# From chunk 8 on, keys and queries are transposed by VectorE in 32x32 blocks, instead of by TensorE with ScalarE's copies

## Chip, cores, metric

One core of one Trainium2 chip. The metric is device time in microseconds; each figure is the median of several runs. The kernel before takes 741.78 us (4 runs, 740.48 to 742.51).

## The reference, cut to what matters

A retention recurrence over 768 positions for 4 batches x 8 heads, then a feed-forward layer on the 3072 tokens it gives:

```python
for t in range(S):
    state = gamma * state + einsum('bhd,bhe->bhde', k[:, :, t], v[:, :, t])
    y[:, :, t] = scale * einsum('bhd,bhde->bhe', q[:, :, t], state)
# ... y becomes x (3072 x 512), then
h = x @ w_in                       # 512 -> 2048
g = h * erf(softplus(h))
out = g @ w_out                    # 2048 -> 512
```

Everything is float32.

## The kernel before

The recurrence is done in chunks of 128 positions, 24 in all (6 a batch). Keys and queries of a chunk are scaled by decay factors (by GpSimd from chunk 7 on), transposed on TensorE into PSUM and copied out by ScalarE:

```python
    def ret_scale(j):                       # K_
        ...
        by = kq_s[:, j % NC, :, :, None].to_broadcast([P, 2, H, D])
        engine = nc.vector if j <= JPC + 2 else nc.gpsimd
        engine.tensor_tensor(KQ[j], KQ[j], by, op=ALU.mult)          # L346

    def ret_transpose(j):                   # T
        for i, (name, store) in enumerate((("k", KT), ("q", QT))):
            p = ret_psum()
            for u in range(HP):             # 4 transposes of 128x128 each
                nc.tensor.transpose(p[:, u, :], ..., ident)          # L355
            store[j] = ret.tile([P, HP, C], F32, name=name + "T")
            nc.scalar.copy(store[j], p)                              # L361
```

The main loop runs over half token pairs ("steps" g = 4 to 23; each does half of the hidden units for 256 tokens, as seven products with sums and differences in place of eight). One chunk of the recurrence (j = g + 2) is threaded through each step as long as there are chunks. The order of one step, for all engines alike:

```python
        hidden_part(g, 1); hidden_part(g, 2)     # part 2 ends with L567 on VectorE
        if put is not None:                      # every second step: results of the
            for step in range(4):                # last token pair go out
                put_part(put, step)              # ScalarE copy, then L637..L646 on VectorE
            put = None
        if more: T(j)
        hidden_part(g, 6)
        if more: S_(j); M(j)                     # scores; mask = L380 on VectorE
        hidden_part(g, 5)                        # reuses the bank that L567 reads
        if more: O_(j)                           # L403/L408, into the banks L380 reads
        hidden_part(g, 7)
        if more: U(j); A(j); ret_scale(j + 1)    # state product, state addition
        ...                                      # x_sums (L534), projections, parts 4, 3
        gate(g)                                  # ScalarE: softplus, then Erf (L451)
        ...                                      # more projections on TensorE
        gated(g); g_sums(g)                      # VectorE: 2 x L470, 4 x L594
```

What one step's `gated` and `g_sums` ask of VectorE is carried out at the start of the next step, when Erf is done.

## Time and profile before

| what | before |
|---|---|
| median | 741.78 us |
| profiled span | 739.9 us |
| TensorE busy | 723.5 us (98%) |
| one main-loop step (from one Erf end to the next) | 29.38 us |

A step's length is the difference of two successive ends of the Erf activation in the timeline. In the kernel before it repeats to 0.01 us from step to step. Two kinds of step must be told apart: "output steps" (odd g from 7 on, with the three VectorE additions L637 to L646 ahead of the mask) and the others. In the kernel before both take 29.38 us, since TensorE is full in both. (Steps whose chunk begins or ends a batch are 0.6 or 0.8 us shorter, as they lack some products.)

### The profile page before, as it was taken

To read this page: it belongs to the slowest core of one execution; us is meant where nothing else is said; L and a number is where in the kernel's file an instruction comes from. 1 tells how busy PE (TensorE), PEld (TensorE's weight loads), DVE (VectorE), ACT (ScalarE), POOL (GpSimd) and SP (SyncE) were. 2 spreads that over 40 slices of the span, in tenths; PEclk is the share of its full clock that TensorE was granted. 3 is DMA by queue.
4 is the path that set the end of the run, shared out by engine and by line. 5 is a ranking of instruction groups with operands and counts; after the bars stand their busy time and mean duration, and the time that the engine had idled before them with its cause. 6 is when DMAs were issued, how large, how long until landed. Compare 5 with 4: busy or idle time off the path is not lost.

```text
span 739.9 us, 11780 instructions
## 1 busy us (share of the span) xinstructions
PE 723.5 (98%) x5260; PEld 609.1 (82%) x5260; DVE 352.4 (48%) x461; ACT 274.3 (37%) x320; POOL 34.9 (5%) x30
## 2 busy tenths in 40 slices
PE   7889999999999999999999999999999999999997
PEld 6644444576999999999999999999999999999995
DVE  3999999955543332531631532433414424243314
ACT  2354562415334144244242341542442423414440
POOL 1000010010101101101001011011010100000000
PEclk9999999999999999999999999999999999999999
DMA  9999653021201201302202022112021000000000
GB/s 190 207 242 233 151 159 114 0 45 57 44 15 29 72 1 43 73 1 43 72 1 43 33 41 43 50 23 45 28 45 38 7 29 2 1 29 1 1 29 28
DMA packets 87522, 42.71 MB, mean 58 GB/s; under 512 B 76208, under 2 KB 76208, under 8 KB 87472
## 3 DMA queue, kind: packets, MB, share of 16 engines
q1 hardware_dynamic: 83920, 41.16, 24.0%
q10 hardware_dynamic: 3552, 0.80, 0.6%
q8 instruction: 41, 0.67, 0.4%
q14 instruction: 9, 0.07, 0.0%
HBM read 35.66 MB, written 6.29 MB: 57 GB/s over the span
## 4 chain that ended last, share of the span: by engine, by line
PE 79%; DVE 12%; DMA 4%; issue 2%; SPq 2%; ACT 1%; DVEq 0%; ACTq 0%
PE hp L551 34%; PE o L611 32%; PE r L368 3%; PE r L408 2%; PE r L355 2%; DVE w_out_sb L199 2%; DVE w_out_sb L201 2%; PE o L494 2%; DMA w_in_sb<-in_moe_w_in_dram 2%; DMA kq<-in_k_dram 2%; PE r L422 1%; DVE w_out_sb L197 1%; PE r L403 1%; DVE w_in_sb L191 1%; DMA v<-in_v_dram 1%
## 5 line engine op out<-in xcount | busy, mean ns | idle before, releaser
L551 PE MATMUL hp<-xs,w_in_sb 128*128 128x128 f32 x1280 | 159.4, 278 | 0.0
L551 PEld LDWEIGHTS hp<-xs,w_in_sb 128*128 128x128 f32 x1280 | 150.5, 192 | 7.0 <-issue 3.6
L611 PE MATMUL o<-w_out_sb,h 128*128 128x256 f32 x640 | 141.6, 379 | 0.0
L470 DVE TENSOR_TENSOR e<-h,e 128x1024 f32<-128x1024 f32 x44 | 51.9, 1221 | 180.0 <-ACT e L451 180.0
L611 PEld LDWEIGHTS o<-w_out_sb,h 128*128 128x128 f32 x640 | 121.6, 190 | 16.5
L551 PE MATMUL hp<-xT,w_in_sb 128*128 128x128 f32 x960 | 113.7, 275 | 0.0
L551 PEld LDWEIGHTS hp<-xT,w_in_sb 128*128 128x128 f32 x960 | 111.9, 192 | 1.9 <-issue 1.0
L611 PE MATMUL o<-w_out_sb,e 128*128 128x256 f32 x480 | 111.8, 382 | 0.9 <-DVE e L470 0.9
L611 PEld LDWEIGHTS o<-w_out_sb,e 128*128 128x128 f32 x480 | 88.2, 190 | 12.6 <-DVE e L470 1.3
L450 ACT ACT_TABLE_LOAD x24 | 30.8, 1283 | 91.2 <-PE o L611 89.1
L481 PE MATMUL hp<-xT,w_in_sb 128*128 128x512 f32 x128 | 58.4, 609 | 0.0
L346 POOL TENSOR_TENSOR kq<-kq,kq_s 128x1024 f32<-128x1024 f32 x17 | 32.7, 1925 | 534.4 <-DMA kq<-in_q_dram 469.8
L574 DVE TENSOR_TENSOR h<-h,hp 128x512 f32<-128x512 f32 x20 | 13.7, 687 | 86.4 <-ACT h L572 86.4
L579 DVE TENSOR_TENSOR h<-h,hp 128x512 f32<-128x512 f32 x20 | 13.7, 687 | 72.3 <-PE hp L551 72.3
L481 PEld LDWEIGHTS hp<-xT,w_in_sb 128*128 128x128 f32 x128 | 24.4, 196 | 28.7 <-issue 27.9
L413 ACT COPY xT<-r 128x256 f32<-128x256 f32 x44 | 14.4, 375 | 78.8 <-PE r L408 78.8
L450 ACT ACTIVATE e<-h 128x2048 f32<-128x2048 f32 x22 | 42.0, 1910 | 0.2
L451 ACT ACTIVATE e<-e 128x2048 f32<-128x2048 f32 x22 | 42.0, 1910 | 0.2
L577 ACT COPY h<-hp 128x512 f32<-128x512 f32 x20 | 11.7, 585 | 72.4 <-PE hp L551 72.4
L380 DVE TENSOR_TENSOR am<-r,causal 128x512 f32<-128x512 f32 x44 | 28.4, 683 | 18.3 <-PE r L368 17.0
L451 ACT ACT_TABLE_LOAD x24 | 30.8, 1283 | 0.4
L355 PE MATMUL r<-ident,kq 128*128 128x128 f32 x176 | 23.5, 275 | 5.8 <-DVE kq L346 5.5
(91 smaller groups left out, 656.3 us busy)
## 6 DMA issues: line engine op xcount, KB each, us to landing
w_out_sb<-in_moe_w_out_dram SPq DMA_DIRECT2D x14, 512.0 KB, 5.2
kq<-in_k_dram SPq DMA_DIRECT2D x24, 256.0 KB, 3.2
v<-in_v_dram SPq DMA_DIRECT2D x24, 256.0 KB, 4.2
w_in_sb<-in_moe_w_in_dram SPq DMA_DIRECT2D x12, 512.0 KB, 7.4
out_dram<-r SPq DMA_DIRECT2D x24, 256.0 KB, 2.3
kq<-in_q_dram SPq DMA_DIRECT2D x21, 256.0 KB, 4.0
w_out_sb<-in_moe_w_in_dram SPq DMA_DIRECT2D x4, 512.0 KB, 8.5
w_in_sb<-in_moe_w_out_dram SPq DMA_DIRECT2D x2, 512.0 KB, 4.1
```

What stands on the lines that cost most here:

```text
L199: nc.vector.scalar_tensor_tensor(lowf, lo, 2.0**-52, lowf, op0=ALU.mult, op1=ALU.mult)
L201: nc.vector.tensor_tensor(lowf, topf, lowf, op=ALU.add)
L346: engine.tensor_tensor(KQ[j], KQ[j], by, op=ALU.mult)
L355: nc.tensor.transpose(p[:, u, :], KQ[j][:, i, 2 * u : 2 * u + 2, :].rearrange("p h d -> p (h d)"), ident,)
L368: nc.tensor.matmul(pp[s][:, hp, :], KT[j][s * D : (s + 1) * D, hp, :], QT[j][s * D : (s + 1) * D, hp, :], start=True, stop=True,)
L380: nc.vector.tensor_tensor(AM[j][:, s], SC[j][s], causal[:, None, :].to_broadcast([P, HP, C]), op=ALU.mult)
L450: nc.scalar.activation(E[g], HS[g], AF.Softplus)
L451: nc.scalar.activation(E[g], E[g], AF.Erf)
L470: nc.vector.tensor_tensor(E[g][:, half], HS[g][:, half], E[g][:, half], op=ALU.mult)
L481: nc.tensor.matmul(p, w_in_of(ft, kk), XC[0][:, kk, :], start=(kk == 0), stop=(kk == n_k - 1))
L551: nc.tensor.matmul(bank[:, u, :], w_in_sb[:, s, IN[a], kk, u * P : (u + 1) * P], XS[m][b][:, kk, :], start=(p in (1, 2, 5) and u == 0 and ...
L611: nc.tensor.matmul(O[m][i][:, half, :], G[g][a][:, u * P : (u + 1) * P], w_out_sb[:, s, OUT[b], u, :], start=i not in started, stop=(s == ...
```

## The change

The intent is to take 8 transposes a chunk off TensorE, the engine that bounds the kernel. VectorE can transpose 32x32 blocks within a tile. If each transfer from memory puts the blocks of a head pair at the right partitions, the block transpose gives exactly the layout that TensorE's transposes gave. Keys are wanted untransposed too (for the state), so they are loaded twice. The decay factors then depend on partition and block instead of on the partition alone, hence a second table `kq_b` and two more GpSimd multiplications in place of half of the old one.

```diff
+    NB = 2 * JPC                                   # 8
+    def load_blocks(to, src):
+        for s, d in itertools.product(range(2), range(2)):
+            part = slice((2 * s + d) * 32, (2 * s + d + 1) * 32)
+            for u in range(HP):                    # 16 transfers of 16 KB
+                nc.sync.dma_start(
+                    to[part, u * C : (u + 1) * C].rearrange("p (a d) -> p a d", d=32),
+                    src[2 * u + s, :, d * 32 : (d + 1) * 32].rearrange("(a p) d -> p a d", p=32),
+                )
     def load(j):
+        if j >= NB:
+            KB[j] = loads.tile([P, HP * C], F32, name="kb", bufs=2)
+            nc.sync.dma_start(KQ[j][:, 0], k[...])             # keys as they were
+            load_blocks(KQ[j][:, 1]..., q[...])                # queries in blocks
+            load_blocks(KB[j], k[...])                         # keys in blocks
...  (load_block_scales, block_scales: the table kq_b, once)
     def ret_scale(j):
+        if j >= NB:
+            nc.gpsimd.tensor_tensor(KQ[j][:, 0], ..., op=ALU.mult)
+            for i, x in enumerate((KB[j], KQ[j][:, 1]...)):
+                by = kq_b[:, j % NC, i, :, :, None].to_broadcast([P, HP, 4, 32])
+                nc.gpsimd.tensor_tensor(x, x, by, op=ALU.mult)     # L394
+            return
     def ret_transpose(j):
+        if j >= NB:
+            for name, store, x in (("k", KT, KB[j]), ("q", QT, ...)):
+                store[j] = ret.tile([P, HP, C], F32, name=name + "T")
+                nc.vector.transpose(store[j]..., x)                # L410
+            return
...  in the loop:
-        if more:
+        if more and j < NB:
             T(j)
...
             U(j); A(j)
-            ret_scale(j + 1)
+            for later in (j + 1, j + 2):
+                if later not in scaled: K_(later)
+            if NB <= j + 1 < NJ: T(j + 1)
+            if j + 3 < NJ: load(j + 3)
...
-        x_sums(g + 1)          # ahead of projection 1, parts 4 and 3
+        x_sums(g + 1)          # behind them, its tile with one buffer instead of two
```

The load of chunk 8 moves behind the weights, from step 2 to the end of step 3. The lines have other numbers: L380 became L440, L403 L463, L408 L468, L470 L530, L551 L611, L567 L627, L594 L654, L611 L671.

More of the change, by code (lines that the diff above doesn't have):

```diff
@@ L82 @@
     ctx.enter_context(tc.manual_schedule())
-    KQ, V = {}, {}
+    KQ, V, KB = {}, {}, {}
+    NB = 2 * JPC
[7 more added lines that the diff above has]
+                )
     def load(j):
@@ L91, in load @@
         now = slice(c * C, (c + 1) * C)
-        for i, src in enumerate((k, q)):
+        if j >= NB:
+            KB[j] = loads.tile([P, HP * C], F32, name="kb", bufs=2)
+            nc.sync.dma_start(KQ[j][:, 0], k[b, :, now, :].rearrange("h p d -> p h d"))
+            load_blocks(KQ[j][:, 1].rearrange("p h d -> p (h d)"), q[b, :, now, :])
+            load_blocks(KB[j], k[b, :, now, :])
+        for i, src in enumerate((k, q) if j < NB else ()):
             queue = nc.scalar if i and j < 3 else nc.sync
@@ L315, in other_scales, with load_block_scales, block_scales @@
         query_scale(slice(1, NC))
+    kq_b = const.tile([P, NC, 2, HP, 4], F32, name="kq_b")
+    by_b = const.tile([P, 2, HP], F32, name="by_b")
+    def load_block_scales():
+        for s, d in itertools.product(range(2), range(2)):
+            part = slice((2 * s + d) * 32, (2 * s + d + 1) * 32)
+            for u in range(HP):
+                nc.sync.dma_start(
+                    kq_b[part, 0, 0, u],
+                    decay_k[:, 2 * u + s : 2 * u + s + 1].rearrange("(a p) h -> p (a h)", p=32),
+                )
+        nc.sync.dma_start(by_b[:, 1], decay_s)
+    def block_scales():
+        nc.vector.reciprocal(by_b[:, 0], by_b[:, 1])
+        nc.vector.reciprocal(kq_b[:, 0, 1], kq_b[:, 0, 0])
+        nc.vector.tensor_scalar(kq_b[:, 0, 1], kq_b[:, 0, 1], unscale, None, op0=ALU.mult)
+        for c in range(1, NC):
+            nc.gpsimd.tensor_tensor(
+                kq_b[:, c], kq_b[:, c - 1], by_b[:, :, :, None].to_broadcast([P, 2, HP, 4]),
+                op=ALU.mult,
+            )
     QT, KT, SC, AM, XC, SU = {}, {}, {}, {}, {}, {}
@@ L342, in ret_scale @@
         scaled.add(j)
+        if j >= NB:
+            nc.gpsimd.tensor_tensor(
+                KQ[j][:, 0], KQ[j][:, 0],
+                kq_s[:, j % NC, 0, :, None].to_broadcast([P, H, D]), op=ALU.mult,
+            )
+            for i, x in enumerate((KB[j], KQ[j][:, 1].rearrange("p h d -> p (h d)"))):
+                x = x.rearrange("p (u a d) -> p u a d", u=HP, d=32)
+                by = kq_b[:, j % NC, i, :, :, None].to_broadcast([P, HP, 4, 32])
+                nc.gpsimd.tensor_tensor(x, x, by, op=ALU.mult)
+            return
         by = kq_s[:, j % NC, :, :, None].to_broadcast([P, 2, H, D])
@@ L351, in ret_transpose @@
         assert j in scaled
+        if j >= NB:
+            for name, store, x in (
+                ("k", KT, KB[j]), ("q", QT, KQ[j][:, 1].rearrange("p h d -> p (h d)"))
+            ):
+                store[j] = ret.tile([P, HP, C], F32, name=name + "T")
+                nc.vector.transpose(store[j].rearrange("p u t -> p (u t)"), x)
+            return
         for i, (name, store) in enumerate((("k", KT), ("q", QT))):
@@ L426, in ret_state @@
             pace(1)
-        if j == 0 or JPC <= j < NJ - 3:
+        if j == 0 or j == JPC:
             load(j + 3)
@@ L529, in x_sums @@
         m = chunk_of(g)
-        xs = ret.tile([P, 4, 2, P], F32, name="xs")
+        xs = ret.tile([P, 4, 2, P], F32, name="xs", bufs=1)
         b11, b12, b21, b22 = (x_quarter(m, d, t) for d in range(2) for t in range(2))
@@ L697 @@
         ],
-        [([], []), ([], [(x_sums, G0)]), ([], [(K_, 6)]), ([], [])],
+        [
+            ([], []),
+            ([(load_block_scales,)], [(x_sums, G0)]),
+            ([], [(K_, 6)]),
+            ([(load, 8)], []),
+        ],
     ]
@@ L738 @@
             A(j)
-            ret_scale(j + 1)
+            if first:
+                block_scales()
+            for later in (j + 1, j + 2):
+                if later not in scaled:
+                    K_(later)
+            if NB <= j + 1 < NJ:
+                T(j + 1)
+            if j + 3 < NJ:
+                load(j + 3)
             j += 1
-        if g + 1 < NG and (g - G0) % 2:
-            x_sums(g + 1)
         if first:
@@ L748 @@
         hidden_part(g, 3)
+        if g + 1 < NG and (g - G0) % 2:
+            x_sums(g + 1)
         if first:
```

## The prediction

> **What bounds the kernel now.** First the page's parts 1 and 2: who is busy, and where in the span.
>
> ```profile
> PE 723.5 (98%) x5260; PEld 609.1 (82%) x5260; DVE 352.4 (48%) x461; ACT 274.3 (37%) x320; POOL 34.9 (5%) x30
> PE   7889999999999999999999999999999999999997
> DVE  3999999955543332531631532433414424243314
> ```
>
> TensorE is full from about the ninth slice of 40 on; VectorE is full before that (it converts weights). The change acts from chunk 8 on. One chunk is done in each step of the main loop, chunk 6 in step 4, so chunk 8 is in step 6 and chunk 23 in step 21: 16 steps of about 29 us in the part where TensorE is full. Whether a microsecond off TensorE comes off the time is read in the chain that ended last, in order of time. Here is one such step of it, from the two hidden products that open it to the next gate:
>
> ```profile
> 322.84 3.57 PE hp L551 x32
> 326.41 0.87 PE r L355 x8
> 327.28 1.79 PE hp L551 x16
> 329.07 1.09 PE r L368 x16
> 330.16 1.98 PE hp L551 x16
> 332.14 1.02 PE r L408 x16
> 333.17 1.98 PE hp L551 x16
> 335.15 0.61 PE r L422 x16
> ```
>
> Nothing but TensorE is in it, end to start. L355 is the eight transposes: 0.87 us of chain a chunk, although a single one is recorded with 273 ns (they are pipelined, 0.109 us apart). ScalarE's copies (L361) are nowhere in this chain, so what ScalarE saves is worth nothing by itself.
>
> What matters then is how close VectorE follows behind. Each step's VectorE chain starts where Erf ends (L451). It is the two gating products (L470), four sums (L594), an addition that frees a PSUM bank (L567), in every second step four output additions (L637 to L646), and the mask (L380). From the timeline of a step with output:
>
> ```profile
> 293.89 2.36 DVE L470 TENSOR_TENSOR e<-h,e 128x1024 f32<-128x1024 f32 x2 [9.26 <-ACT e L451]
> 298.83 0.68 DVE L567 TENSOR_TENSOR h<-h,hp 128x512 f32<-128x512 f32 x1
> 301.52 2.05 PE L551 MATMUL hp<-xs,w_in_sb 128*128 128x128 f32 x16
> 301.80 1.28 DVE L380 TENSOR_TENSOR am<-r,causal 128x512 f32<-128x512 f32 x2
> 303.50 0.67 PE L403 MATMUL r<-qT,state 64*64 64x128 f32 x16
> ```
>
> VectorE runs 9.19 us without a gap, from 293.89 to the end of the mask at 303.08. L403, which writes into the two banks that the mask reads, starts at 303.50. So the reserve there is 0.42 us. The product at 301.52 needs L567 (end 299.51): reserve 2.0 us. These reserves are the heart of the matter, as the Erf end is set by TensorE's work **before** the removed transposes and the consumers stand **after** them.
>
> **What the Trainium skill says.** (1) TensorE: Matmul & The Clock Gate, Part 4: a transpose on TensorE is a matmul against an identity and took about 275 ns inside a kernel. The trace has 273 ns, but shows that its cost in a stream is 109 ns. (2) VectorE: DVE Perf Modes, The three transpose paths: VectorE transposes 32x32 blocks only, SBUF to SBUF. No row of the kernel before shows one; that it does a four-byte element at one per cycle is an assumption of mine, so I take the 0.69 us of other 128x512 VectorE rows. (3) SBUF — State Buffer, Who interferes with whom: a VectorE instruction with two SBUF inputs and a GpSimd instruction that reads SBUF exclude each other for the whole instruction. The trace agrees: GpSimd's scaling ran 1.90 us from 307.78 and the first L534 behind it took 1.53 us instead of 0.42; and with one at 102.60 an L191 took 2.80 us instead of 1.23:
>
> ```profile
> 102.60 2.13 POOL L346 TENSOR_TENSOR kq<-kq,kq_s 128x1024 f32<-128x1024 f32 x1 [27.03 <-DMA kq<-in_q_dram]
> 103.02 2.80 DVE L191 SCALAR_TENSOR_TENSOR w_in_sb<-w_in_sb 128x1024 uint32<-128x1024 uint32 x1
> ```
>
> (4) DMA: Bandwidth & Descriptors, Anatomy of one DMA: a fixed 2 us or so a transfer, mostly completion. The page's part 6 has 2.3 us for outputs; the 4 KB table took 1.7.
>
> **The change part by part.**
> Removed from TensorE: 16 chunks x 0.87 us = **13.9 us of chain** (1.9% of 741.7, so even whole it falls just short of 2%).
> Removed from ScalarE: 32 copies x 0.585 = 18.7 us, off the path: 0.
> Added on VectorE: 32 block transposes x 0.69 (estimate) = 22 us. In program order they stand after the state addition, with the next chunk's operands, where VectorE idles (in the waits, L470 waits 9.3 us a step for Erf, L579 up to 4.5). Even at twice the length they fit: 0. The four sums for the next token pair (L534) move behind L579, into the same idle time: 0.
> Added on GpSimd: three multiplications of 128x512 instead of one of 128x1024. Five of 128x8 took 1.32 us, so 0.26 each, and 1024 take 1.90; 512 are then an estimated 1.08 us, 3.2 us a chunk. GpSimd itself has the time.
> Added on the load queue: 34 transfers a chunk instead of 3. Successive issues are 0.42 us apart:
>
> ```profile
> 335.84 0.37 SPq L95 DMA_DIRECT2D kq<-in_k_dram  x1
> 336.26 0.57 SPq L95 DMA_DIRECT2D kq<-in_q_dram  x1
> ```
>
> The outputs' are as far apart (two in 0.83). 34 x 0.42 = 14.3 us of a 28 us step, so loads still finish more than a step ahead of use: no stall from data. The one-time loads of 4-byte scales (17 issues) end long before they are needed.
>
> **Less for the mask.** In the 8 steps with output (odd chunks 9 to 23) L403 would start at 303.50 - 0.87 = 302.63, yet the mask ends at 303.08. TensorE waits 0.45 and keeps 0.42 of the 0.87. In the other 8 steps the mask starts when the scores are done, and moves with them: 0.87 in full. Sum: 8 x 0.87 + 8 x 0.42 = **10.3 us**, so **731.4 us** if nothing else happens.
>
> **Rivals.** *A: GpSimd's later scaling falls on VectorE's tight chain.* The issues begin 0.07 us after the state products end (335.77). The last block of keys is the 33rd issue, 32 x 0.42 = 13.4 us later, and lands some 2 us after that: at 351.3. The next L470 starts at 351.24. So two GpSimd multiplications (keys, then queries) become ready just as VectorE starts its six two-input instructions in SBUF, 5.1 us in all. In the kernel before the load landed about 4 us after the state products (GpSimd at 340.30), where VectorE had nothing tight; that is lost. From the pair above, 1.9 us of GpSimd cost VectorE 1.57, some 0.3 less than its length; two of 1.08 then cost about 1.6. A step with output has no reserve left and loses all of it; the others lose what exceeds 1.1 (the 2.0 less 0.87), so 0.5. The loads of chunks 9 to 23 hit steps 5 to 19: step 5 still has its transposes, and the two steps after a sequence's last chunk are spared since that chunk has no state products and its load starts earlier. 7 x 1.6 + 5 x 0.5 = 13.7 us: **745 us**. With one of the two colliding (0.8 us): 7 x 0.8 = 5.6, so **737 us**. Against it: it hangs on the issue time. At under 0.35 us an issue the keys land 2.2 us earlier and GpSimd is done before L470; over 0.57, after the sums. And the scaling may have to wait until VectorE pauses; then it costs nothing.
> *B: the free case*, 731.4, if small transfers issue faster than the large ones seen here. For: a 32-partition transfer carries an eighth of the pieces. Against: the 256 KB loads with 1024 pieces show 0.37 and the outputs 0.41, so pieces seem not to set it.
> *C: loads become the bound.* 4096 pieces of 128 bytes more a chunk; the queues are at 14% in this part. If an issue took 0.8 us, 34 would take 27 us of a 28 us step, and transposes would begin to wait for keys: 755 or more. The semaphores allow eight transfers in flight, so a landing would have to take over 3.4 us to slow issue; small ones should not.
> *D: all of the 13.9 us and a little more*, 727 or less, if VectorE's chain gets quicker. I see nothing that makes it so.
>
> **Range and chances.** B 30% at 731.4, one collision 25% at 737, both 40% at 745, C 5% at 755: mean 739; I take 738, a little toward the free case, as the person who moved L534 out of the way may have looked at VectorE's order. Eight in ten from 729 to 748. Faster by over 2% means below 726.9: 0.05. Slower means above 756.5: 0.04.
>
> **What would show each step right or wrong.** The L355 group must fall from 176 to 48 on PSUM tile r, and the chain lose its 0.87 us rows. In steps with output a new wait of L403 for L380 of about 0.45 us must appear (8 of them) even without collisions. If A holds, L470 or L594 show means above 1221 and 690 ns, the late scalings start within a few tenths of L470, and waits for L380 grow to about 2 us, with some of L551 for L567 (0.5 us). If GpSimd's late pair is done 2 us ahead of L470, or starts after the sums, A is wrong and the time is near 731. Wrong as a whole I would be if block transposes take several us each and push L579 or L470 out, if TensorE waits for KT or QT, or if the issue takes longer than a step.

## The result, and the profile after

The changed kernel takes **745.05 us** (4 runs, 744.81 to 745.24), against 741.78 before: a ratio of 1.0046 (95% interval 1.0028 to 1.0063). Here and below a ratio is the mean time of one kernel's runs over that of the other's of the same rounds, so it is not quite the ratio of the medians quoted. A gain of 0.5% was forecast; a loss of 0.4% was measured.

Busy times and the chain's shares by engine, from the page of the kernel after:

```profile
PE 712.3 (96%) x5132; PEld 595.3 (80%) x5132; DVE 388.4 (52%) x496; ACT 256.9 (35%) x288; POOL 65.2 (9%) x67
PE 64%; DVE 18%; ACT 12%; issue 3%; DMA 2%; DVEq 0%; ACTq 0%
```

TensorE has 128 instructions less and 11 us less to do, yet its idle time grew by more: 743.0 - 712.3 = 30.7 us against 739.9 - 723.5 = 16.4. The chain of waits, which in the main loop held TensorE alone, now runs through VectorE and ScalarE as well. Here is the opening of step 10 in it, as it stands in order of time:

```profile
323.52 5.37 PE hp L611 x48
328.91 0.69 DVE h L654
329.59 0.61 DVE h L627
330.20 0.04 issue
330.25 2.05 PE hp L611 x16
```

The 0.87 us of transposes are gone (three hidden products in one row of 48), but the next product waits for L627, the addition that frees its PSUM bank. The view of who waited for whom, for 200 to 650 us (columns: total us, times, longest), has TensorE's new waits:

```profile
PEld r L463 <- DVE am L440: 10.7, 14, 1.1
PEld hp L611 <- DVE h L627: 8.1, 13, 0.7
PE r L463 <- DVE am L440: 7.7, 14, 0.9
PE hp L611 <- DVE h L627: 5.7, 13, 0.6
```

In the same stretch before there was none of either kind. (PEld and PE wait together; the two rows of a pair are not to be added.) The timeline of step 9, an output step, shows why VectorE is late:

```profile
293.36 2.36 DVE L530 TENSOR_TENSOR e<-h,e 128x1024 f32<-128x1024 f32 x2 [9.26 <-ACT e L511]
295.97 1.38 POOL L394 TENSOR_TENSOR kb<-kb,kq_b 128x512 f32<-128x512 f32 x1 [13.79 <-DVE e L530]
296.48 1.42 DVE L654 TENSOR_TENSOR h<-h,e 128x512 f32<-128x512 f32 x1
297.31 1.49 POOL L394 TENSOR_TENSOR kq<-kq,kq_b 128x512 f32<-128x512 f32 x1
297.82 1.53 DVE L654 TENSOR_TENSOR h<-e 128x512 f32<-128x512 f32 x1
300.61 2.05 PE L611 MATMUL hp<-xs,w_in_sb 128*128 128x128 f32 x16 [0.42 <-DVE h L627]
302.85 1.28 DVE L440 TENSOR_TENSOR am<-r,causal 128x512 f32<-128x512 f32 x2
303.59 0.43 PE L463 MATMUL r<-qT,state 64*64 64x128 f32 x2 [0.93 <-DVE am L440]
```

GpSimd's two multiplications fall among VectorE's sums; two of these take 1.42 and 1.53 us instead of 0.69, and TensorE waits 0.42 us for the bank and 0.93 for the mask. (The row names L530 as what released GpSimd, as it ended last before it; but the last piece of keys landed at 295.55 us, so GpSimd started when its data was there.) Over the loop (grouped by line and shape, 205 to 617 us) the second of the sums has a mean of 1225 ns, where the same row before had 692:

```profile
L654 DVE TENSOR_TENSOR h<-h,e 128x512 f32<-128x512 f32 x14 | 17.1, 1225 | 0.5
L410 DVE STREAM_TRANSPOSE kT<-kb 128x512 f32<-128x512 f32 x14 | 9.9, 704 | 0.0
```

```profile
L594 DVE TENSOR_TENSOR h<-h,e 128x512 f32<-128x512 f32 x14 | 9.7, 692 | 0.5
```

(The first fence is the kernel after, the second the kernel before.) The block transposes themselves take 0.67 to 0.70 us (0.69 was estimated).

By steps: output steps take 30.6 to 30.7 us instead of 29.38, the others 28.9 to 29.1 (28.51 in step 20, which no late scaling meets; steps 9, 10, 15 and 16, at a batch's end or start, are shorter). From the Erf of step 4 to that of step 21 the loop grew from 498.50 to 502.74 us. But from the Erf of step 1 to that of step 4, where weights are converted, time fell from 93.90 to 92.70 us. -1.2 + 4.24 = +3.0, and the spans differ by 3.1.

### The profile page after: what moved, and what is told of

It reads as the page before. It is cut to its first block, busy times and chain, and to the rows that moved or that the text cites. A ratio compares the mean times of both kernels' runs of the same rounds, so it can differ in the third digit from the quotient of the medians. Undisturbed runs are those within 1.5% of the kernel's fastest.

```text
span 743.0 us, 12213 instructions
## 1 busy us (share of the span) xinstructions
PE 712.3 (96%) x5132; PEld 595.3 (80%) x5132; DVE 388.4 (52%) x496; ACT 256.9 (35%) x288; POOL 65.2 (9%) x67
## 4 chain that ended last, share of the span: by engine, by line
PE 64%; DVE 18%; ACT 12%; issue 3%; DMA 2%; DVEq 0%; ACTq 0%
PE hp L611 23%; PE o L671 21%; PE o L554 7%; DVE h L654 5%; PE hp L541 5%; DVE e L530 4%; ACT e L511 4%; ACT e L510 4%; PE r L468 3%; ACT L510 2%; ACT L511 2%; DVE am L440 2%; DMA kq<-in_q_dram 2%; PE r L482 1%; PE r L463 1%
## 5 line engine op out<-in xcount | busy, mean ns | idle before, releaser
L611 PE MATMUL hp<-xs,w_in_sb 128*128 128x128 f32 x1280 | 159.3, 278 | 5.7 <-DVE h L627 5.7
L611 PEld LDWEIGHTS hp<-xs,w_in_sb 128*128 128x128 f32 x1280 | 150.5, 192 | 13.5 <-DVE h L627 8.1
L671 PE MATMUL o<-w_out_sb,h 128*128 128x256 f32 x640 | 141.6, 379 | 0.0
L530 DVE TENSOR_TENSOR e<-h,e 128x1024 f32<-128x1024 f32 x44 | 54.2, 1273 | 167.0 <-ACT e L511 167.0
L671 PEld LDWEIGHTS o<-w_out_sb,h 128*128 128x128 f32 x640 | 121.6, 190 | 16.5
L611 PE MATMUL hp<-xT,w_in_sb 128*128 128x128 f32 x960 | 113.7, 275 | 0.0
L611 PEld LDWEIGHTS hp<-xT,w_in_sb 128*128 128x128 f32 x960 | 111.9, 192 | 1.9 <-issue 1.0
L671 PE MATMUL o<-w_out_sb,e 128*128 128x256 f32 x480 | 111.8, 382 | 0.9 <-DVE e L530 0.9
L671 PEld LDWEIGHTS o<-w_out_sb,e 128*128 128x128 f32 x480 | 88.1, 190 | 12.6 <-DVE e L530 1.3
L541 PE MATMUL hp<-xT,w_in_sb 128*128 128x512 f32 x128 | 56.9, 596 | 0.0
L639 DVE TENSOR_TENSOR h<-h,hp 128x512 f32<-128x512 f32 x20 | 13.7, 687 | 67.8 <-PE hp L611 67.8
L654 DVE TENSOR_TENSOR h<-e 128x512 f32<-128x512 f32 x40 | 37.6, 939 | 0.7
L394 POOL TENSOR_TENSOR kb<-kb,kq_b 128x512 f32<-128x512 f32 x16 | 19.4, 1214 | 203.7 <-DMA kb<-in_k_dram 133.5
L387 POOL TENSOR_TENSOR kq<-kq,kq_s 128x512 f32<-128x512 f32 x16 | 16.7, 1042 | 166.8 <-DMA kq<-in_k_dram 166.8
```

The source lines that it names most:

```text
L387: nc.gpsimd.tensor_tensor(KQ[j][:, 0], KQ[j][:, 0], kq_s[:, j % NC, 0, :, None].to_broadcast([P, H, D]), op=ALU.mult,)
L394: nc.gpsimd.tensor_tensor(x, x, by, op=ALU.mult)
L530: nc.vector.tensor_tensor(E[g][:, half], HS[g][:, half], E[g][:, half], op=ALU.mult)
L541: nc.tensor.matmul(p, w_in_of(ft, kk), XC[0][:, kk, :], start=(kk == 0), stop=(kk == n_k - 1))
L611: nc.tensor.matmul(bank[:, u, :], w_in_sb[:, s, IN[a], kk, u * P : (u + 1) * P], XS[m][b][:, kk, :], start=(p in (1, 2, 5) and u == 0 and ...
L654: nc.vector.tensor_tensor(x[to], x[a], x[b], op=ALU.add if plus else ALU.subtract)
```

## The experiments

Theory: GpSimd's two late multiplications hold up VectorE's instructions with two inputs in SBUF just as its tight chain runs, and the wait passes on to TensorE. Rivals: the block transposes or the moved sums burden VectorE; the 128-byte loads disturb; GpSimd's work costs VectorE wherever it falls.

The step times are the sharpest measure, so here they are for all runs (output step 7, other step 8, and the loop from the Erf of step 4 to that of step 21; worked out from Erf ends in each timeline):

| run | median us | before, same rounds | output step | other step | loop |
|---|---|---|---|---|---|
| before | 741.78 | | 29.38 | 29.38 | 498.50 |
| after | 745.05 | 741.78 | 30.68 | 29.00 | 502.74 |
| no_scale | 730.59 | 741.28 | 29.01 | 28.50 | 488.50 |
| gate_pool | 729.30 | 741.28 | 29.01 | 28.50 | 488.52 |
| mask_first | 732.43 | 741.28 | 29.13 | 29.12 | 492.08 |
| gate_mask | 726.38 | 741.28 | 28.50 | 28.51 | 484.52 |
| half_scale | 734.57 | 741.33 | 29.86 | 28.50 | 494.15 |
| double_t | 727.00 | 741.33 | 28.51 | 28.50 | 484.52 |
| before_pool | 771.66 | 741.33 | 32.16 | 30.56 | 527.90 |
| before_pool2 | 749.36 | 741.64 | 30.57 | 29.38 | 506.85 |
| before_loads | 749.94 | 741.33 | 29.38 | 29.38 | 498.49 |
| before_loads2 | 741.89 | 741.64 | 29.38 | 29.38 | 498.50 |
| before_hold | 738.80 | 741.64 | 29.38 | 29.38 | 498.50 |

### no_scale: the late multiplications taken away

```diff
             nc.gpsimd.tensor_tensor(KQ[j][:, 0], ...)
-            for i, x in enumerate((KB[j], KQ[j][:, 1]...)):
-                ...
-                nc.gpsimd.tensor_tensor(x, x, by, op=ALU.mult)
             return
```

> The changed kernel without GpSimd's two late multiplications (the keys and queries in blocks stay unscaled, so the result is wrong on purpose); loads, block transposes and the later sums all stay. Theory (GpSimd's late scaling holds up VectorE's tight chain): about 13.7 us come back, so 731 us; waits for the gating chain before the products vanish, a wait of about 0.45 us of the first state product for the mask stays in each of 8 output steps. Rival 1 (the block transposes or the later sums burden VectorE): still about 745. Rival 2 (the 128-byte loads disturb): still about 745.

Measured: 730.59 us, ratio 0.9852 (0.983 to 0.9873); the result is wrong. Both rivals that leave loads, transposes and moved sums at fault are out: all of these are still there. The loop falls by 502.74 - 488.50 = 14.2 us (13.7 predicted). One wait of TensorE for another engine is left in the stretch from 200 to 650 us, the one foretold for output steps (there, L436 is the mask and L459 the state product):

```profile
PEld r L459 <- DVE am L436: 2.5, 8, 0.3
```

Eight times, in output steps only; these take 29.01 us, 0.5 more than the others' 28.50.

### gate_pool: the same multiplications at another time

```diff
+            if NB <= j + 1 < NJ: T(j + 1)
             for later in (j + 1, j + 2):
-                if later not in scaled:
+                if later not in scaled and later < NJ:
+                    if later > NB:
+                        nc.gpsimd.tensor_copy(tick, KT[later - 1][:, 0, :1])
                     K_(later)
-            if NB <= j + 1 < NJ: T(j + 1)
```

> The changed kernel, right results, with GpSimd's scaling of chunk j+2 held until VectorE has transposed chunk j+1 (a one-column copy on GpSimd reads what the transpose wrote), so the same multiplications run where VectorE idles. Theory: the same 731 us as without the multiplications, within 1.5. Rival 1 or 2: about 745. A further rival, that GpSimd's work costs VectorE wherever it falls: 740 or more.

Measured: 729.30 us, ratio 0.9832 (0.9817 to 0.9847), right results, and the steps equal those of no_scale to 0.01 us. So the cost of GpSimd's work is all in **when** it runs, that is, in what VectorE does at that time. This is the repair of the change: one column copied, and a loss of 0.4% becomes a gain of 1.7%.

### mask_first: more reserve instead of less delay

```diff
         if put is not None:
-            for step in range(4):
-                put_part(put, step)
-            put = None
+            put_part(put, 0)
         ...
             S_(j); M(j)
+        if put is not None:
+            for step in range(1, 4):
+                put_part(put, step)
+            put = None
         hidden_part(g, 5)
```

> The changed kernel with the three output additions on VectorE after the mask instead of ahead of it; GpSimd's late scaling stays where it falls. Theory: the mask of an output step now has the reserve of the other steps, so both kinds of step lose only what the addition that frees the PSUM bank is late (about 0.5 us in some 14 steps): 727.8 + 7 = 735 us. If the mask were not the wait that counts: 745.

Measured: 732.43 us, ratio 0.9874 (0.9857 to 0.989). Output steps fall from 30.68 to 29.13, the same as the others. The order of the mask was what made output steps lose all of the delay. The bank's wait remains, about 0.6 us in most steps; 735 was expected, but the gain of the weight stage (below) was not in that sum.

### gate_mask: both

> Both edits together, right results. Theory: all 16 x 0.87 us are kept, 741.7 - 13.9 = 728 us, with no wait of TensorE for VectorE left in the main loop. If something else holds part of the gain back, more than 731.

Measured: **726.38 us**, ratio 0.9802 (0.9781 to 0.9822), right results: 2.0% under the kernel before, the best of all versions. Every ordinary step takes 28.51 us = 29.38 - 0.87. The loop's gain is 498.50 - 484.52 = 13.98 us; 13.9 was the whole of the transposes. The chain in order of time is TensorE alone again, without L355:

```profile
290.31 5.36 PE hp L612 x48
295.67 1.09 PE r L429 x16
296.76 1.98 PE hp L612 x16
298.74 0.60 PE r L464 x16
```

and GpSimd's multiplications stand behind the transpose, where VectorE has nothing to do that reads two inputs from SBUF:

```profile
303.60 0.70 DVE L411 STREAM_TRANSPOSE kT<-kb 128x512 f32<-128x512 f32 x1
304.37 0.18 POOL L814 COPY tick<-kT 128x1 f32<-128x1 f32 x1 [24.69 <-DVE kT L411]
305.51 1.05 POOL L395 TENSOR_TENSOR kb<-kb,kq_b 128x512 f32<-128x512 f32 x1
```

The block transposes of the queries, which read one input, run beside GpSimd here in 15 steps and take 0.67 us, as in the kernel after, where none ran beside GpSimd.

### half_scale: half the dose

```diff
+                if i == 0:
                     nc.gpsimd.tensor_tensor(x, x, by, op=ALU.mult)
```

> The changed kernel with one of GpSimd's two late multiplications (the queries in blocks stay unscaled, wrong on purpose). Theory, a dose of the same cause: one multiplication costs VectorE about 0.8 us, which the 7 output steps that are hit lose whole and the others (reserve 1.1) not at all: 730.6 (measured with none) + 7 x 0.8 = 736 us. If the cause were not the number of multiplications but that the load lands late, 745.

Measured: 734.57 us, ratio 0.9909 (0.9893 to 0.9926). Its output is wrong, which doesn't matter for the time. The output step of the table is 29.86 - 29.01 = 0.85 us longer than with none, the others unchanged at 28.50; the loop is 494.15 - 488.50 = 5.65 us longer (5.6 expected). That the other steps lose nothing to 0.85 us and 0.5 to twice that is the mark of a reserve of about 1.1 us.

### double_t: does the block transpose cost anything?

gate_mask with each block transpose done twice.

```diff
+                for _ in range(2):
                     nc.vector.transpose(...)
```

> The kernel with held GpSimd scaling and the mask first (726.4 us measured), with each block transpose done twice. Theory: transposes stand where VectorE idles, so 32 more of 0.69 us (22 us of VectorE time) cost nothing: 726.4, within 1.5. If VectorE's transposes cost time, up to 22 us more.

Measured: 727.00 us, ratio 0.9805; loop 484.52, equal to the last digit. 32 more transposes are free. VectorE's load was not the trouble.

### before_pool and before_pool2: the collision put into the kernel before

TensorE's transposes stay; two unused GpSimd multiplications start when Erf ends.

```diff
         nc.scalar.activation(E[g], E[g], AF.Erf)
+        if 5 <= g <= 18:
+            nc.scalar.copy(tick, ident[:, :1])
+            for _ in range(2):
+                nc.gpsimd.tensor_tensor(scratch, scratch, tick.to_broadcast([P, 512]), op=ALU.mult)
```

> The kernel before, TensorE's transposes kept, with two unused GpSimd multiplications of 128x512 that start when Erf ends (they wait for a one-column ScalarE copy behind it) behind gates 5 to 18. Theory: VectorE's chain is 1.6 to 2 us late in 14 steps; the 7 output steps have a reserve of 0.42 and lose 1.2 to 1.6 us each, the other 7 a reserve of 2.0 and lose nothing: 741.3 + 8 to 11 = 750 to 752 us. A rival that needs the block transposes or the small loads for the loss: 741.

Measured: 771.66 us, ratio 1.0407 (1.0388 to 1.0426): a miss in size. The timeline shows three multiplications in the window, not two: GpSimd works in order, and the kernel's own scaling of a later chunk (128x1024) had come to stand behind mine. As a measurement it is good all the same. Output steps lose 32.16 - 29.38 = 2.78 us, the others 1.18 (step 19, with a fourth multiplication in the window, loses 4.48). With the reserves read in the profile of before (0.42 and 2.0) both give one delay of VectorE: 2.78 + 0.42 = 3.20 and 1.18 + 2.0 = 3.18 us. before_pool2 puts the kernel's own scaling ahead:

```diff
-            ret_scale(j + 1)
+            for later in range(j + 1, j + 4):
+                if later not in scaled: ret_scale(later)
```

> As the last try on the kernel before (two unused GpSimd multiplications started when Erf ends, behind gates 5 to 18), but with the kernel's own scaling ahead of them in GpSimd's order, so that only two multiplications and not three stand in the way. Theory: VectorE is then late by 1.64 us as in the changed kernel; output steps lose 1.64 - 0.42 = 1.2 us each in 7 steps, the others nothing (reserve 2.0): main-loop steps of 30.6 and 29.4 us, 741.3 + 8.5 = 750 us. Rival (the loss needs the changed layout or loads): steps of 29.4, 741.

Measured: 749.36 us, ratio 1.0109 (1.0095 to 1.0122). Steps of 30.57 and 29.38 us. The loss can thus be made without block transposes and without small loads. The pair of gating products in this run, on the timeline, beside GpSimd:

```profile
294.25 3.21 DVE L479 TENSOR_TENSOR e<-h,e 128x1024 f32<-128x1024 f32 x2 [9.26 <-ACT e L454]
294.37 3.98 POOL L458 TENSOR_TENSOR scratch<-scratch,tick 128x512 f32<-128x512 f32 x2 [8.58 <-ACT tick L456]
```

3.21 us where 2.36 is usual: the first of the two took its usual 1.23 us, the second 2.06, so GpSimd was let in between two VectorE instructions that stand back to back.

### before_loads and before_loads2: the small loads alone

```diff
+        if j >= NB:
+            KB[j] = loads.tile([P, 2, HP * C], F32, name="kb", bufs=1)    # nobody reads it
+            load_blocks(KB[j][:, 0], q[b, :, now, :])
+            load_blocks(KB[j][:, 1], k[b, :, now, :])
```

with the moved, single-buffered x_sums as well.

> The kernel before with the 32 block loads a chunk into a tile that nobody reads, and with the later place of the token sums and their single buffer, as in the change. Theory: neither is on the path: 741 us, within 1.5. Rival (the small loads or the moved sums cost time): 743 or more.

Measured: 749.94 us, ratio 1.0113: a miss, though the loop is unchanged (498.49). The loss is in the weight stage, 103.04 us from the Erf of step 1 to that of step 4 instead of 93.90: my version kept the load of chunk 8 at its old place, so 32 issues (96.26 to 114.67 us on the load queue) stood ahead of a piece of weights that went out at 115.26 instead of 102.41. before_loads2 takes the change's places:

```diff
-        if j == 0 or JPC <= j < NJ - 3:
+        if j == 0 or j == JPC:
             load(j + 3)
...                                     # chunk 8 at the end of step 3, the others behind A(j)
```

> The kernel before with the 32 unread block loads a chunk, now at the change's places (chunk 8 behind the weights, the others at the end of a step). Theory: the 8.6 us that the first try lost arose while weights are loaded, as its loads stood ahead of weight pieces; here no step changes: 741, or 740 as a scaling of GpSimd leaves the weight stage. Rival (small loads cost by themselves): 745 or more.

Measured: 741.89 us, ratio 1.0005 (0.9991 to 1.0018). The small loads and the moved sums cost nothing where the change put them. The change was right to move chunk 8.

### before_hold: the gain at the start

```diff
+            if first:
+                nc.gpsimd.tensor_copy(tick, state[:, 0, :1])
             ret_scale(j + 1)
```

> The kernel before with GpSimd's scaling of chunks 7 and 8 held until the fourth step (a one-column copy that reads the state). Theory: in the kernel before the two run in the stage that VectorE bounds and hold it up (2.80 us instead of 1.23 for one L191); without them the stage ends about 1.2 us sooner, as it does in the changed kernel: 740.1 us. If that stage gained its 1.2 us from something else in the change: 741.3.

Measured: 738.80 us, ratio 0.9966 (0.9953 to 0.998), so a gain of 2.5 us by the means (2.8 by the medians) rather than 1.2. GpSimd's first scaling is now at 157 us, the loop is unchanged, and the weight stage takes 92.70 us, to the hundredth what the kernel after takes. Other traces in which GpSimd scales in that stage have 93.90 to 95.02 us there (the kernel before, before_loads2; 95.08 in before_pool2), so the gain is 1.2 to 2.4 us by trace, depending on what GpSimd falls on. In the changed kernel the same gain came about by accident: GpSimd, working in order, waits for the table `kq_b`, which VectorE fills only in step 4.

## Why the prediction was wrong

**The mechanism and its terms were right.** The loop's change, split into three differences between runs (they add up by construction), each beside its predicted term:

| term | predicted | measured | from |
|---|---|---|---|
| transposes off the chain | -13.9 | -13.98 | gate_mask against before |
| mask wait in 8 output steps | +3.6 | +4.0 | no_scale against gate_mask |
| GpSimd's late scaling, both colliding | +13.7 | +14.2 | after against no_scale |
| loop | +3.4 | +4.24 | after against before |
| weight stage | 0 | -1.2 | Erf of step 1 to step 4, before and after |

The delay of VectorE was to be 1.6 us. It was 30.68 - 29.01 = 1.67 in the output step of the table. The others that were hit lost 0.34 to 0.62 (0.5 predicted).

**The step that failed is the overlap, as "Range and chances" weighed it.** Rival A, that both late multiplications fall on VectorE's chain, was worked out at 745 us and then counted at 40%. It came in all twelve steps that A named: GpSimd's first multiplication started 1.9 to 3.3 us behind L530, inside VectorE's 5.1 us of two-input instructions, and the two cost the loop 14.2 us (after against no_scale). The prediction averaged A with B (30% at 731) and the single collision (25% at 737) and leaned toward the free case because whoever moved L534 "may have looked at VectorE's order". That is no evidence from the profile. The mix turned a loss into a forecast gain of 3.7 us, a time that no single course gave.

**What should have weighed more.** The 30% for B rested on small transfers issuing faster than 0.42 us. They issued slower: the 33 issues up to the last keys took 15.3 to 17.0 us from the first to the last, 0.48 to 0.53 each, though each had an eighth of a large load's pieces. The last keys were then issued about 16 us after the state products, not 13.4, and most landed 1.6 to 1.9 us later (2.9 at most). By the prediction's own sums nothing between 0.35 and 0.57 us an issue would have missed the window. The other hope, that GpSimd would have to wait until VectorE pauses, is refuted by before_pool2 and by the pair of rows at 102 us that the prediction itself shows.

**Where luck helped.** That A's 745 us is the measured time is partly luck: the loop grew by 0.8 us more than A's terms say, and the weight stage, not foreseen, took 1.2 off. A also had GpSimd start at about L470's start. It started 2 to 3 us later, so in the twelve steps the sums (L654) were lengthened, and the gating products (L530, mean 1303 ns) in steps 10 and 16 only. The cost was the same because the window is 5.1 us wide. The wait of about 2 us for the mask came in two parts, 10.7 / 7 = 1.5 us an output step for the mask and about 0.6 for the bank ahead of it.

**Misjudged beside it.** Step 10, behind a batch's last chunk, was to be spared; it lost 28.25 - 27.91 = 0.34 us by no_scale's step. Its load did start early, 19 us ahead of L530 (303.90 and 323.14), but 33 issues took 17 us of that, and GpSimd began at 322.82. Step 16 was spared as said: GpSimd began 1.0 us ahead of L530, and one product was lengthened by 0.85 us, within the reserve of 1.1. And the weight stage's gain was not seen: the profile showed GpSimd at 102.60 holding up L191, and the changed order of GpSimd, which takes that away, could be read from the program. One small misreading has no consequence: the page's row shows PE at 9 from the fourth slice on, not from the ninth.

**Right as put:** no wait for data, no cost of the block transposes or of the moved sums, nothing from ScalarE's saved copies.

## What to carry to other kernels

Before an operation is taken off the busiest engine, read how far the next engine follows behind on each path that crosses the removed piece: the removed time is paid only up to that reserve (here 0.42 of 0.87 us in every second step), and each new delay beyond it is passed on in full. Work that "has room" on another engine must also be placed in time: a GpSimd multiplication that runs as soon as its load lands runs wherever the load happens to put it, and a one-column copy that ties it to the right moment turned +0.4% into -1.7%. When a rival is worked out to a number and its conditions are in the profile, forecast it or its opposite, not the average.

## What the Trainium skill lacked or had wrong

- SBUF — State Buffer, Who interferes with whom, says that whoever starts first has the shared path for a whole instruction and the other blocks. The runs agree, but the page does not say outright who goes next when both engines have work queued. In before_pool2 they took turns, instruction by instruction: beside the first L479 (1.23 us, from 294.25) GpSimd's first multiplication took 2.00 us (1.05 for this shape in gate_mask, undisturbed), then the second L479 took 2.06 instead of 1.22, GpSimd's second 1.90, and the next sum 1.41 instead of 0.69. Step 10 of the changed kernel shows the same turns. A GpSimd instruction of 1.05 us cost VectorE 0.7 to 0.85 us, less than its whole length.
- DMA: Bandwidth & Descriptors, Issuing engines are not separate DMA queues, calls the issue time "usually small relative to the DMA itself". For 16 KB transfers it was 0.48 to 0.53 us each against a median of 1.7 to 1.8 us from issue to landing, and 33 of them in a row (15.3 to 17.0 us) decided when the data was ready.
- No page has a measured time of a VectorE block transpose of four-byte elements (Vector Engine (DVE) Microarchitecture Reference, 3.8, has a rate for the block transpose, one element per cycle and lane, and no time): 128x512 took 0.67 to 0.70 us, like other VectorE instructions of that shape (0.69).
